# One written order for the first four chunks of a chunked recurrence followed by a two-matrix layer

## The chip, the cores and the metric

The kernel runs on one core of a Trainium2 chip. A time is device microseconds (us) for one execution of the whole program; smaller is better. TensorE is written PE in the profile, VectorE DVE, ScalarE ACT, GpSimd POOL and SyncE SP. PE's weight loads have their own row, PEld. SP computes nothing here: it issues DMAs, one after another, in the order of its instruction list.

## The reference

Two stages follow each other. The first is a recurrence over 768 tokens, with a 40 by 40 state for each of 4 batches and 8 heads:

```python
for t in range(S):
    y[:, :, t] = np.einsum('bhd,bhde->bhe', rt, state)
    Sa = np.einsum('bhde,bhe->bhd', state, at)
    state_decay = state * wt[:, :, None, :] - np.einsum('bhd,bhe->bhde', Sa, bt)
    state = state_decay + np.einsum('bhd,bhe->bhde', vt, kt)
```

Its output, turned to 3072 tokens by 320 channels, goes through a layer of two matrices with a SiLU between:

```python
h = x @ w_in                            # 320 x 2048
g = h * (1.0 / (1.0 + np.exp(-h)))
return (g @ w_out).astype(np.float32)   # 2048 x 320
```

The recurrence's inputs are float32. The two matrices arrive as float64, which the kernel has to turn into float32 itself.

## The kernel before, in words

**Chunks.** The 768 tokens are cut into twelve chunks of 64. A chunk has two units `m`, each with two of the four batches. Within a chunk the recurrence becomes matrix products around the inverse of a triangular 64 by 64 matrix for each head and batch; from chunk to chunk only the state `GV` is carried.

**What a chunk needs.** `prepare` scales it (two scans and a reciprocal on DVE for each unit, L335 and L336; key products on POOL) and forms the `scores` (PE products `pm`, evicted by DVE into `sb`, L286). The scores go through DRAM (`md`) into a layout with one matrix per partition (`mi`). `inverse` then solves row by row on DVE: a product `tmp` (L419) and a sum into `XI` (L426) for every row. The result returns through DRAM (`xd`) into `XT`. `merge` turns it (L463) and completes the inverse of size 64 from blocks with PE products (`corners`, `complete`, `first`, `second`). Chunks 0 and 1 are inverted one by one on 64 partitions, the later ones in pairs on 128 partitions; for chunks 0 to 3 the row solve goes to blocks of 16, later to blocks of 32.

**The chain of a chunk** has six steps for each unit: `keys` (products `pt`), `right` (`pr`), `solve` (`pu`, `pw`), `read` (`pl`, masked by DVE into `vl`, L722), `write` (`pgy`, then DVE's update of `GV`, L761 and L765, and `yx`, L770) and `turn` (`GT`). `keyed` makes a further masked product for the chunk (L308). The outputs of two chunks go to DRAM as `xs`.

**The layer.** For two chunks, 512 tokens, `moe` gives a queue of steps: `first` (products `ph` with `w_in`, L813 and L818, SiLU on ACT at L820) and `second` (products `po` with `w_out`, L825). For the first pair `first` is cut in two halves of 256 tokens, so that chunk 0's tokens can go ahead of chunk 1's. Such steps fill PE between the dependent products of a chain.

**The weights.** 40 pieces (`pieces`), each a float64 block of 128 partitions by 256 numbers. `load_weights` brings piece n into a free room; `weights(n)` does two bit operations of piece n on DVE (L178, L179), gives three conversions to ACT (L180 to L182), and finishes piece n - 1 with three DVE operations (L187, L189, L190). The first 20 pieces use five rooms inside parts of the weight tensors that are not written yet and the tile `room`; pieces 20 to 29 have three rooms, and the last ten the tiles `mi`, `tmp` and `room`. The tile tag `room` also holds `stage`, the keys of every odd chunk from 5 on (`staged`, `load`); `stack` copies them to where `keyed` wants them.

**Order.** Without further word the order within each engine is chosen when the program is built, from the order in which the steps are written and the buffers' lifetimes. `in_order` adds a dependency that costs nothing on the chip but fixes an instruction behind the last one given the same name: `"moe"` for PE, `"vector"` for DVE, `"sync"` for SP. Before, DVE's line is written for chunks 0 and 1's scaling, masks, inversions and pieces 0 to 3; SP's line is written at the very start, dropped (`del issued["sync"]`) and taken up again ahead of chunk 4. PE's line is kept for the layer's products, and from chunk 4 on (`mark["pair"]`, read by `product`) for all products. Chunks 0 to 3 are spread by `weave`, which mixes lists of steps evenly: the chain, the layer's steps, and the conversions. From chunk 4 a loop over pairs of chunks (L1025) states every step's place; `take(n)` runs the next n steps of the layer's queue.

Of the kernel before, what the change touches and what calls it, by code (L numbers as in the profile page):

```python
# [41 lines left out]
def kernel(  # L42
# [97 lines left out]
    def load_weights(done):  # L140

        while len(rooms) < NW:
            n = len(rooms)

            if n < NW // 2:
                place = ("wi0", "wi1", "wo0", "wo1", "room")[n % 5]
            elif n < NW * 3 // 4:
                place = ("wo0", "wo1", "room")[(n - NW // 2) % 3]
            else:
                place = ("mi", "tmp", "room")[(n - NW // 2) % 3]  # L150
            if taken.get(place, -1) > done:
                return
            taken[place] = n
            at = int(place[-1]) if place[0] == "w" else None
            if place[:2] == "wi":
                rooms[n] = wi_s[:, at, DF // 2 : DF // 2 + 4 * WS].bitcast(I32)
            elif place[:2] == "wo":
                at = NF * DM // 2 + 4 * WS * at
                rooms[n] = wo_f[:, at : at + 4 * WS].bitcast(I32)
            else:  # L160
                rooms[n] = sb.tile([128, 4 * WS], I32, name="room", tag=place)
            for lo, hi, src in pieces[n][1]:
                raw = rooms[n][lo:hi, 0 : 2 * WS]
                send(nc.sync, raw.rearrange("p (i x) -> p i x", x=256) if len(src.shape) == 3 else raw, src)
            if n < 3:
                return
# [6 lines left out]

    def weights(n, pin=lambda x: x, more=True):

        if n < NW:
            lo, hi, e, f = parts(n)
# [23 lines left out]
    def in_order(x, line="moe"):  # L201

        if line in issued:
            behind(x, issued[line])
        issued[line] = x.ins

    class Unit:
# [61 lines left out]
    def between(u, s):  # L269
# [15 lines left out]
        for j in range(2):  # L285
# [5 lines left out]
            )  # L291
            if u.n < 2:
                in_order(x, "vector")

    def keyed(u):
# [10 lines left out]
        for j in range(2):  # L306
# [6 lines left out]
            )  # L313
            if u.n == 0:
                in_order(x, "vector")

# [8 lines left out]
    def pre(u, md):  # L325
        def scale():
            u.W = sb.tile([128, Q, C + 1], F32, name="W", bufs=6)
            R = u.w[:, :, 1 : C + 1]
            pin = partial(in_order, line="vector") if u.n < 2 else lambda x: x
            if "pair" in mark and u.n % 2 == 0:  # L330

                pin = lambda x: behind(x, mark["row" if u.m == 0 else "across"])
# [61 lines left out]
    def inverse(md, N, queue, lo=0, hi=128):  # L394
# [18 lines left out]

        pin = partial(in_order, line="vector") if hi - lo == 64 else lambda x: x

# [26 lines left out]
    def merge(n, xd, queue):  # L442
# [14 lines left out]

        pin = partial(in_order, line="vector") if n < 2 else lambda x: x

# [138 lines left out]
    def chain(u, xs):  # L598
# [109 lines left out]
        def read():  # L708
# [12 lines left out]
            for j in range(2):  # L721
                nc.vector.tensor_tensor(  # L722
                    out=u.vl[:, :, j, D:],
                    in0=pl[j].rearrange("p (q t) -> p q t", q=Q),
                    in1=ml.unsqueeze(1).to_broadcast([128, Q, C]),
                    op=ALU.mult,
                )

        def write():
# [27 lines left out]
            for be in range(0 if last else 2):  # L757
                for j in range(2):
                    J = slice(DP * j, DP * j + DP)
                    g = gv[J, j, P * be : P * be + P]  # L760
                    nc.vector.tensor_tensor(out=g, in0=gy[be][J, :, 0:D], in1=g, op=ALU.add)  # L761
            for j in range(0 if last else 2):
                J = slice(DP * j, DP * j + DP)
                g = gv[J, j]
                nc.vector.tensor_tensor(  # L765
                    out=g, in0=g, in1=u.W[J, :, C : C + 1].to_broadcast([DP, Q, D]), op=ALU.mult
                )
            yx = sb.tile([128, P, 2, C], F32, name="yx")
            for be in range(2):
                nc.vector.tensor_tensor(  # L770
                    out=yx[:, :, be], in0=gy[be][:, :, D:], in1=u.W[:, P * be : P * be + P, 0:C], op=ALU.mult
                )
            at = 2 * C * (NM * (u.n % 2) + u.m)
# [10 lines left out]
    def moe(n0, xs, apart=False):  # L784
# [63 lines left out]
        for half in range(2):  # L848
            for c in range(2 if apart else 1):
                T = slice(W * c, W * c + W) if apart else slice(0, 2 * W)  # L850
                steps += [partial(first, T, NF // 4 * half + i) for i in range(NF // 4)]
                steps += [partial(second, half, b) for b in range(T.start // 128, T.stop // 128)]
        return fetch, steps
# [42 lines left out]
    for t in GVf + GT + XT + [x[DP * j + 32 : DP * j + DP, :, 1] for x in VUT for j in range(2)]:  # L896
        nc.gpsimd.memset(t, 0.0)
    def pinned(n, more=True):
        weights(n, partial(in_order, line="vector"), more)

# [10 lines left out]
    load_weights(-1)  # L911
    convert = [partial(weights, n) for n in range(NW + 1)]
    xs = dr.tile([DM, 4 * NM * C], F32, name="xs", bufs=2)
    steps = prepare(0)
    run([steps[i] for i in (0, 1, 4, 5)])
    pinned(0, False)
    pinned(1, False)
    run([steps[i] for i in (2, 6, 3, 7)])
# [13 lines left out]
    for u in units[0]:  # L932
        load_r(u)
    chains = {0: [chain(u, xs) for u in units[0]]}
    run(rows[1:18])
    for u in units[0]:
        keyed(u)
    run([x[i] for i in range(2) for x in chains[0]])
    run([next_steps[i] for i in (1, 2, 5, 6, 3, 7)])
    pinned(2)  # L940
    pinned(3)
    for u in units[1]:
        load_v(u)
    merge0 = late.pop(0)
    run(merge0[0:1])
    rows = invert(1, 1)
    run(rows[0:5] + merge0[1:2] + rows[5:9] + merge0[2:3] + rows[9:18] + merge0[3:])
    del issued["sync"]
    steps = [x for pair in zip(*[x[2:] for x in chains[0]]) for x in pair]
    steps[6:6] = late.pop(1)  # L950
    steps[2:2] = [partial(keyed, u) for u in units[1]]
    weave(steps, convert[4:12])
    for u in units[1]:
        load_r(u)
    for u in units[2] + units[3]:
        load(u)
    fetch, queue = moe(0, xs, True)
    fetch(0)
    steps = [x for pair in zip(*[chain(u, xs) for u in units[1]]) for x in pair]
    weave(steps[0:4], convert[12:14])  # L960
    issued["moe"] = mark["right"].ins
    weave(steps[4:], queue[0:4], convert[14:21])
    del queue[0:4]
    fetch(1)
    ahead = [prepare(n) for n in (2, 3)]
    weave(
        queue[0:8],
        [x[i] for x in ahead for i in (0, 5, 1, 6, 2, 7, 4, 9, 3, 8)] + [partial(keyed, u) for u in units[2]] + invert(3),
        convert[21:31],
    )  # L970
    del queue[0:8]
    for n in range(2, 4):
        for u in units[n]:
            load_v(u)
            load_r(u)
        for u in units[n + 2]:
            load(u)
        if n % 2 == 0:
            xs = dr.tile([DM, 4 * NM * C], F32, name="xs", bufs=2)
        steps = [x for pair in zip(*[chain(u, xs) for u in units[n]]) for x in pair]  # L980

        now = {2: 4, 3: 5}[n]
        x = prepare(n + 2)
        if n == 2:
            weave(steps[0:4], queue[0:1], [x[i] for i in (0, 5, 1, 6)], convert[31:34])
            scores = [x[i] for i in (2, 4, 7, 9, 3, 8)]
        else:
            weave(steps[0:4], queue[0:1], [x[i] for i in (0, 5, 2, 7, 1, 6, 4, 9, 3, 8)])
            scores = [partial(stack, u) for u in units[n + 2]]
        rows = invert(n + 2)  # L990
        merges = rows[35:]
        weave(
            steps[4:6] + late.pop(n, []) + [partial(keyed, u) for u in units[n + 1]] + steps[6:],
            queue[1:now],
            scores + rows[0:36],
            convert[34:] if n == 2 else [],
        )
        del queue[0:now]
    for u in units[6]:
        load(u, "bk")  # L1000
    fetch, more = moe(2, xs)
    fetch(0)
    queue += more

    def each(what, n, *x):
        for u in units[n] if n < NN else []:
            what(u, *x)

    def take(n):
        x = queue[0:n]  # L1010
        del queue[0:n]
        run(x)

    def start(n):

        x = [chain(u, xs) for u in units[n]]
        return [[y[i] for y in x] for i in range(len(x[0]))]


    mark["pair"] = True  # L1020
    issued["sync"] = mark["mi"]
    each(load_v, 4)
    each(load_r, 4)
    take(8)
    for n in range(4, NN, 2):  # L1025
        xs = dr.tile([DM, 4 * NM * C], F32, name="xs", bufs=2)
        keys, right, solve, read, write, turn = start(n)
        x = prepare(n + 2)
        later = late.pop(n)
        run(merges[1:2] + keys + merges[2:3] + right)  # L1030
        each(load_v, n + 1)
        each(load, n + 2, "a")
        each(load, n + 3)
        take(1)
        run(solve[0:1] + later[0:2] + [x[i] for i in (0, 5, 1, 6) if x])
        take(1)
        run(solve[1:2] + later[2:3] + [x[i] for i in (2, 7, 3, 8) if x] + read)
        each(load_vut, n + 1)
        take(1)
        run([x[i] for i in (4, 9) if x] + write)  # L1040
        each(load_vl, n + 1)
        each(keyed, n + 1)
        take(1)
        x = prepare(n + 3)
# [10 lines left out]
        rows = invert(n + 3)  # L1055
        merges = rows[35:]
        run(rows[0:1] + [x[i] for i in (3, 8) if x])
# [170 lines left out]
```

## Time and profile before

| | |
|---|---|
| Median of 3 runs | 901.02 us (898.65 to 906.04) |
| The profiled execution | 901.06 us, its span 899.2 us |
| PE busy / PEld busy | 778.9 (87%) / 552.9 (61%) us |
| DVE busy | 557.9 (62%) us |
| ACT / POOL busy | 297.4 (33%) / 151.4 (17%) us |
| Granted PE clock, mean | 0.946 of full speed |
| A reciprocal L336 / a row product of size 31 by 31, L419 | 3347 / 1160 ns |
| One `po` product L825 / one `ph` product L813, mean | 448 / 549 ns |

The span is the time from the first to the last instruction; some 1.9 us lie around it. A line of the timeline gives start, duration, engine, source line, operation, output and inputs, and in brackets how long the engine had been idle and what ended that. A line of the waits gives engine and product, what it waited for, and the total, the number of times and the longest in us. Most PE products of the chains carry L264, the line of the helper `product`; the tile's name tells them apart.

### The profile page before, as it was taken

To read this page: it belongs to the slowest core of one execution; us is meant where nothing else is said; L and a number is where in the kernel's file an instruction comes from. 1 tells how busy PE (TensorE), PEld (TensorE's weight loads), DVE (VectorE), ACT (ScalarE), POOL (GpSimd) and SP (SyncE) were. 2 spreads that over 40 slices of the span, in tenths; PEclk is the share of its full clock that TensorE was granted. 3 is DMA by queue.
4 is the path that set the end of the run, shared out by engine and by line. 5 is a ranking of instruction groups with operands and counts; after the bars stand their busy time and mean duration, and the time that the engine had idled before them with its cause. 6 is when DMAs were issued, how large, how long until landed. Compare 5 with 4: busy or idle time off the path is not lost.

```text
span 899.2 us, 25358 instructions
## 1 busy us (share of the span) xinstructions
PE 778.9 (87%) x10914; PEld 552.9 (61%) x10914; DVE 557.9 (62%) x1084; ACT 297.4 (33%) x689; POOL 151.4 (17%) x156
## 2 busy tenths in 40 slices
PE   2145689896898997999998999999999989999995
PEld 2135677674786853875746857648757468574643
DVE  9979889885439598176896295982768912510000
ACT  2234358532622322514025342226140243311120
POOL 7312024200202201303102240113031000000001
PEclk9999869996759998999999999999999999999998
DMA  7875646744325542444613627325424021102001
GB/s 154 167 147 142 150 130 150 166 106 107 90 59 128 105 110 47 115 108 87 145 34 62 157 64 158 93 48 117 96 56 122 16 61 40 42 23 57 1 1 33
DMA packets 240151, 82.99 MB, mean 92 GB/s; under 512 B 207136, under 2 KB 231968, under 8 KB 240032
## 3 DMA queue, kind: packets, MB, share of 16 engines
q1 hardware_dynamic: 219488, 69.96, 34.8%
q10 hardware_dynamic: 20544, 11.34, 4.7%
q8 instruction: 87, 1.43, 0.7%
q14 instruction: 32, 0.26, 0.1%
HBM read 67.11 MB, written 14.16 MB: 90 GB/s over the span
## 4 chain that ended last, share of the span: by engine, by line
PE 45%; DVE 19%; DMA 3%; SPq 2%; issue 1%; ACT 1%; POOL 0%; POOLq 0%; ACTq 0%; DVEq 0%
PE po L825 14%; PE ph L813 9%; DVE tmp L419 7%; DVE XI L426 7%; PE pgy L264 4%; PE pl L264 3%; PE ph L818 3%; PE pm L264 2%; SPq L217 2%; PE pt L264 2%; PE pr L264 2%; PE po L264 2%; PE pq L264 2%; PE pu L264 2%; DVE GV L761 1%
## 5 line engine op out<-in xcount | busy, mean ns | idle before, releaser
L825 PE MATMUL po<-wo_s,gts 128*128 128x320 f32 x768 | 224.8, 448 | 17.1 <-ACT gts L820 10.8
L825 PEld LDWEIGHTS po<-wo_s,gts 128*128 128x128 f32 x768 | 145.2, 194 | 82.7 <-ACT gts L820 14.7
L813 PE MATMUL ph<-xt,wi_s 128*128 128x512 f32 (+1 forms) x448 | 182.2, 549 | 2.2 <-ACT ot L834 1.4
L813 PEld LDWEIGHTS ph<-xt,wi_s 128*128 128x128 f32 x448 | 82.1, 192 | 82.3 <-issue 67.9
L820 ACT ACTIVATE gts<-ph 128x512 f32<-128x512 f32 (+1 forms) x112 | 54.6, 531 | 161.1 <-PE ph L818 160.4
L722 DVE TENSOR_TENSOR vl<-pl,ml 128x512 f32<-128x512 f32 x48 | 30.9, 685 | 113.0 <-PE pl L264 77.6
L419 DVE TENSOR_TENSOR tmp<-XI,mi 64x2 f32<-64x2 f32 (+40 forms) x169 | 85.5, 506 | 8.8 <-DMA mi<-md 3.9
L841 POOL TENSOR_TENSOR ot<-gts,ot 128x320 f32<-128x320 f32 x24 | 21.8, 907 | 358.1 <-ACT gts L839 352.9
L336 DVE RECIPROCAL w<-W 128x512 f32<-128x512 f32 x24 | 80.3, 3347 | 1.3
L426 DVE TENSOR_REDUCE XI<-tmp 64x2 f32<-64x2 f32 (+40 forms) x169 | 77.0, 455 | 5.2
L264 PE MATMUL pq<-XT,sb 32*32 32x32 f32 (+1 forms) x1280 | 34.9, 207 | 32.6 <-DVE XT L463 21.1
L818 PE MATMUL ph<-xt,wl_s 64*128 64x512 f32 (+1 forms) x224 | 56.9, 585 | 0.0
L264 PE MATMUL pm<-a,kb 64*64 64x64 f32 x1280 | 41.5, 244 | 16.9 <-POOL kb L366 15.5
L264 PEld LDWEIGHTS pq<-XT,sb 32*32 32x32 f32 (+1 forms) x1280 | 31.6, 131 | 38.7 <-issue 16.0
L363 POOL TENSOR_TENSOR a<-a,W 64x512 f32<-64x512 f32 x32 | 39.5, 1236 | 75.4 <-DMA a<-in_aT 52.2
L1084 DVE TENSOR_SCALAR bad<-pb 1x1 int32<-1x1 f32 x1 | 0.1, 147 | 83.4 <-PE pb L1083 83.4
L264 PEld LDWEIGHTS pm<-a,kb 64*64 64x64 f32 x1280 | 38.1, 156 | 21.2 <-POOL kb L366 15.7
L839 ACT COPY gts<-po 128x320 f32<-128x320 f32 x24 | 10.2, 425 | 121.8 <-PE po L825 98.0
L264 PEld LDWEIGHTS pl<-r,vut 64*128 64x128 f32 x768 | 45.4, 189 | 4.7 <-ACT vl L650 2.1
L264 PE MATMUL pl<-r,vut 64*128 64x64 f32 x768 | 46.5, 274 | 2.0 <-ACT vl L650 2.0
L264 PE MATMUL pt<-ident,kb 128*128 128x128 f32 x192 | 29.1, 313 | 21.2 <-DVE a L308 21.2
L348 POOL TENSOR_TENSOR kb<-kb,w 128x512 f32<-128x512 f32 x20 | 24.8, 1238 | 131.9 <-DVE w L336 118.6
(108 smaller groups left out, 1060.7 us busy)
## 6 DMA issues: line engine op xcount, KB each, us to landing
kb<-in_bT SPq DMA_DIRECT2D x48, 128.0 KB
vut<-in_vT SPq DMA_DIRECT2D x48, 128.0 KB
r<-in_rT SPq DMA_DIRECT2D x24, 256.0 KB
w<-in_wT SPq DMA_DIRECT2D x45, 128.0 KB
kb<-in_kT SPq DMA_DIRECT2D x44, 128.0 KB
a<-in_aT SPq DMA_DIRECT2D x32, 128.0 KB
vl<-in_v SPq DMA_DIRECT2D x48, 80.0 KB
xs<-yx ACTq DMA_DIRECT2D x48, 80.0 KB
```

The lines of the kernel that those rows point to most:

```text
L264: x = what(*x, **y)
L336: pin(nc.vector.reciprocal(R, u.W[:, :, 1 : C + 1]))
L348: nc.gpsimd.tensor_tensor(out=u.kb[:, :, 1], in0=u.kb[:, :, 1], in1=R, op=ALU.mult)
L363: nc.gpsimd.tensor_tensor(out=u.a[J, j], in0=u.a[J, j], in1=u.W[J, :, 0:C], op=ALU.mult)
L419: x = nc.vector.tensor_tensor(out=part, in0=X[L, :, t + 1 : N, t + 1 : N], in1=M[L, :, t, t + 1 : N].unsqueeze(2).to_broadcast([hi - lo, I ...
L426: x = nc.vector.tensor_reduce(out=X[L, :, t + 1 : N, t], in_=part, axis=AX.X, op=ALU.add)
L722: nc.vector.tensor_tensor(out=u.vl[:, :, j, D:], in0=pl[j].rearrange("p (q t) -> p q t", q=Q), in1=ml.unsqueeze(1).to_broadcast([128, Q, C ...
L813: in_order(nc.tensor.matmul(ph[n], lhsT=wi_s[:, k, at : at + 128], rhs=xt[:, k, :], start=k == 0, stop=False))
L818: in_order(nc.tensor.matmul(ph[n], lhsT=wl_s[R, i, :], rhs=xt[R, 2, :], start=False, stop=True))
L820: nc.scalar.activation(out=place(2 * i + n)[:, T], in_=ph[n], func=AF.Silu)
L825: in_order(nc.tensor.matmul(po[:, 0:DM], lhsT=place(f)[:, b * 128 : b * 128 + 128], rhs=wo_s[:, NF // 2 * half + f, :], start=f == 0, stop ...
L841: nc.gpsimd.tensor_tensor(out=ot4, in0=rest, in1=ot4, op=ALU.add)
```

## The change

Line numbers in the diff are those of the file before and after.

1. The order of PE, DVE and SP is written out from chunk 0. `mark["pair"]` is set before chunk 0's chain, so all products follow the written line of PE. A new `mark["front"]` holds until chunk 2's chain begins; while it does, `vec` puts each of DVE's steps, conversions too, into the line `"vector"`. SP's line is no longer dropped.
2. The weaves of chunks 0 to 3 are gone. Chunks 0 and 1 have a written list; chunks 2 and 3 run through the loop over pairs, which now starts at 2. `cv(n)` calls `weights(n)` at stated places.
3. `second` of the first pair comes after both halves of `first`.
4. The last ten pieces use two rooms, `mi` and `room`, and none is loaded into them until the row steps of chunks 2 and 3 have been written (`mark["rows"]`).
5. In the loop's first turn the loads of chunk 5 (`each(load, n + 3)`), `stage` among them, come after the last conversion.

```diff
@@ load_weights
-                place = ("mi", "tmp", "room")[(n - NW // 2) % 3]
+                place = ("mi", "room")[n % 2]
+                if "rows" not in mark:
+                    return
@@ new
+    def vec(x):
+        if "pair" not in mark or "front" in mark:
+            in_order(x, "vector")
+        return x
@@ moe: second behind both halves of first
-                steps += [partial(second, half, b) for b in range(T.start // 128, T.stop // 128)]
+            steps += [partial(second, half, b) for b in range(4)]
@@ the front, from chunk 0's chain to chunk 1's inversion
+    mark["pair"] = mark["front"] = True
+    keys, right, solve, read, write, turn = start(0)
+    run(rows[1:18])
+    each(keyed, 0)
+    run(keys + right)
+    cv(2)
...
+    first, rows = late.pop(0), invert(1, 1)
+    run(first[0:1] + rows[0:1])
+    cv(4)
+    run(first[1:2] + rows[1:6] + first[2:3] + rows[6:12] + first[3:5] + rows[12:17])
+    cv(5)
+    each(load, 3, "bk")
+    run(rows[17:18])
+    x = prepare(2)
+    run(solve + x[0:1])
+    cv(6)
+    then = late.pop(1)
+    run(then[0:2] + read)
...
+    run(keys + right)
+    each(load_v, 2)
+    each(load, 3, "a")
+    each(load, 4, "bk")
...
+    take(1)
+    run([y[4], y[9]] + turn)
+    rows = invert(3)
+    run(rows[0:1])
+    each(keyed, 2)
+    cv(14, 15, 16)
+    take(1)
+    cv(17)
+    weave(rows[1:17], [partial(take, 1)] * 3)
+    mark["rows"] = True
+    run(rows[17:19])
+    cv(18, 19, 20)
+    take(2)
+    cv(21, 22)
+    run(rows[19:20])
+    take(1)
+    merges = rows[20:]
+    del mark["front"]
@@ the loop over pairs
-    for n in range(4, NN, 2):
+    for n in range(2, NN, 2):
...
-        each(load, n + 3)
+        if n > 2:
+            each(load, n + 3)
         take(1)
+        if n == 2:
+            cv(*range(23, 30))
...
+        if n == 2:
+            cv(*range(30, 36))
...
         each(keyed, n + 1)
+        if n == 2:
+            cv(*range(36, NW + 1))
+            each(load, n + 3)
         take(1)
```

## The prediction

> **What bounds the kernel now.** I read the slices of the page first, then busy time by stage, then waits, then the timeline around the inversions.
>
> The slices, 22.5 us each; rows TensorE, VectorE and TensorE's granted clock:
>
> ```profile
> PE   2145689896898997999998999999999989999995
> DVE  9979889885439598176896295982768912510000
> PEclk9999869996759998999999999999999999999998
> ```
>
> VectorE is full over the first nine slices, TensorE from about the fifteenth on. The end of the program is TensorE alone. So the span is TensorE's work plus its holes, and the holes lie early. By stage (span, then busy us of TensorE, its weight loads, VectorE, ScalarE, GpSimd; clock, DMA):
>
> ```profile
> 0.00:125.00 125.00, 53.92 (x1480) 50.34 (x1481) 112.34 (x230) 43.99 (x104) 39.44 (x48) 0.92 0.69 157
> 125.00:205.00 80.00, 74.94 (x933) 57.58 (x929) 70.85 (x156) 48.19 (x123) 15.51 (x13) 0.95 0.52 124
> 205.00:265.00 60.00, 46.62 (x1262) 38.76 (x1260) 22.80 (x53) 24.25 (x58) 7.18 (x8) 0.63 0.36 90
> 265.00:350.00 85.00, 79.67 (x943) 55.76 (x942) 71.92 (x143) 21.28 (x51) 13.34 (x14) 0.98 0.41 94
> 357.00:804.00 447.00, 437.25 (x6032) 302.55 (x6033) 273.80 (x500) 143.14 (x319) 67.61 (x65) 0.98 0.37 83
> 804.00:889.00 85.00, 84.89 (x274) 47.04 (x272) 0.83 (x3) 13.12 (x27) 5.16 (x6) 1.00 0.09 23
> ```
>
> Chunks 0 and 1 (0 to 125) cost 71 us of TensorE's idling, 205 to 265 another 13 and a clock of 0.63: there chunks 2 and 3 are merged, VectorE is busy only 23 of 60 us, and both wait for weights:
>
> ```profile
> PE po L825 <- DVE wo_s L190: 6.3, 2, 3.7
> DVE room L178 <- DMA room<-in_w_out: 12.4, 6, 3.3
> ```
>
> From 357 TensorE misses 10 us in 447. So only what is done before chunk 4's inverse arrives can change the time much. Its path:
>
> ```profile
> 205.58 0.39 SPq L217 DMA_DIRECT2D room<-in_w_out  x1
> ...
> 208.60 0.29 DVE L178 TENSOR_SCALAR room<-room 128x256 int32<-128x256 int32 x1 [2.41 <-DMA room<-in_w_out]
> ...
> 286.15 1.49 POOL L359 TENSOR_TENSOR stage<-stage,W 128x512 f32<-128x512 f32 x1 [2.18 <-DVE W L335]
> 295.58 0.91 PE L264 MATMUL pm<-stage,kb 64*64 64x64 f32 x32
> 296.56 0.76 DVE L286 TENSOR_TENSOR sb<-pm,ms 128x256 f32<-128x256 f32 x2 [2.04 <-PE pm L264]
> 310.00 0.14 DVE L419 TENSOR_TENSOR tmp<-XI,mi 128x1 f32<-128x1 f32 x1
> 355.98 0.31 PE L264 MATMUL pq<-XT,sb 32*32 32x32 f32 x2 [3.68 <-DVE XT L463]
> ```
>
> A weight piece takes 3.0 us from issue to first use. Chunk 5's keys (`stage`) were loaded long before; its scores end at 297.3, the row steps begin at 310.0, and their result is used at 356.5 (the middle of its two first uses, 355.98 and 357.02).
>
> **What the Trainium skill says.** "Perfetto Trace Analysis", Tensor Engine Instruction: ACT, DVE and GpSimd are strict FIFO. So a conversion that waits for its load holds all VectorE work written behind it; the 2.41 us above agrees. "DMA: Bandwidth & Descriptors", Anatomy of one DMA: any semaphore wait happens on the issuing sequencer before dispatch. So a load that waits for its room holds every later load of SyncE; the 18.08 us that three `room` issues took from 215.88 agree. "TensorE: Matmul & The Clock Gate", Why this matters for your kernels: gaps above some 3 us put the array back to half clock; slices of 0.50 follow such gaps here (215 to 235, 245 to 265).
>
> **Part by part.**
>
> *Pinned row steps of chunk 1.* Before, they ran from 63.4 to 92.2, mixed with conversions and a reciprocal of 3.35. Alone they take what chunk 0's took, 30.8 to 43.8: 13 us; with `qq` (0.5) and the addition (0.9) they end near 76, 16 us sooner. SyncE in its written order has piece 9's load (free only after conversion 5, near 79) and eight `kb` loads at 0.65 ahead of chunk 1's fetch: issued 86 to 87.5, transposes end near 91 instead of 110.4. Price: chunk 0's `vl` and `GV` are now queued behind these transposes and end near 112 instead of 106.7. Chunk 1's `pr` comes near 125 instead of 131.
>
> *Fewer conversions ahead of the inversion of chunks 2 and 3.* From 112 VectorE has three scale steps (4.65 each: 14.0), ten conversions (two at 0.28, three at 0.42, 1.8: 18.0), two scores (2.8), `vl` (2.6), `GV` and `yx` (6.2), `keyed` (2.8): 46.4, and some 8 of waiting for chunk 2's scores, which TensorE now runs behind chunk 1's second solve. Rows begin near 167 and end near 181 instead of 205.6. **Lead: 24 us.**
>
> *What eats the lead.* In the built order VectorE has, between rows and chunk 2's transposes, conversions of pieces 20 to 23, whose loads are issued after the fetches of `XT`, pieces 22 and 23 only when 19 and 20 are done. Copy to first use was 10 us before (205.6 to 215.7), so chunk 3's transposes are near 191, and three more piece times (3.0 of load, and conversion) put chunk 2's near 201 to 204. Then 9 us of conversions and a scale step stand ahead of chunk 2's `qq` (213), and `qq` of chunk 3, behind chunk 2's solve in TensorE's written order, stops VectorE from 217 to about 230. Pieces 25 and up are queued on SyncE behind eight `GV` and four `a` loads that wait for chunk 2's `pr`. From 30 on there are two rooms, not three: load 3.0, conversion 1.8 and ScalarE's 1.4 make some 6.5 per pair. `vl` of chunk 2 stands behind piece 33. I put the end of chunk 2's `GV` at 265.5, against 277.2: lead **11.7**.
>
> *The added wait that decides.* `stage` of chunk 5 has the same memory as `room`, and is now loaded after piece 39. VectorE's list from chunk 2's `GV` to piece 39: two scale steps with reciprocals 9.5, sixteen `GT` transposes at 0.43 6.9, `keyed` and `yx` 3.6, four conversions 7.2, some 1 of waiting: 28, to 293.5. Load 3.1; GpSimd's product, two copies and key product 1.3, 1.2, 1.24: 300.4 for the first unit; with the first unit's other product the second follows 5.0 later, 305.4; scores and eviction 1.8: **307.2 against 297.3**. TensorE's order has chunk 3's read and write and four `ph` steps behind these scores; it stands from about 282 (`keyed` of chunk 3 near 270, then its `pr`, two `ph` steps and the two solves, some 12). Then four matmul steps of 2.6, 3.8, 2.6, 5.5 and VectorE's `GV`, `keyed`: 20.5, rows from 327.7; undisturbed they take 39 less 5.7 of `GV` work that was mixed in: 33.3, to 361; and 7.2 as before (349.3 to 356.5): **368.2 against 356.5, +11.7**.
>
> *MoE work put off.* Counted in the trace up to 357: `po` x144 of 16 a step and `ph` of 24 steps, thus 29 steps of the queue taken. The new order has taken 11 before its loop and 16 in the first turn: 27. Two are late, one `ph` of 512 columns (3.63+1.06) and one `po` (4.50): **9.2**. They fall into the tail, which has no hole to hide them.
>
> *Nothing charged:* the hint-only dependencies of the written order; they cost no instruction. Removing `tmp` as a room is in the 6.5 per pair. If that cover is wrong it shows as piece time.
>
> Sum: profiled execution 901.06 (span 899.2, 1.9 around it; the median of the three runs is 901.02) +11.7+9.2 = **922**.
>
> Unknown costs: the lead at chunk 2's write, from 0 (11.7 later than reckoned: 934) to the full 24 (12.3 earlier: 910); piece time in two rooms, from the 3.0 seen to the 5.1 between 208.60 and 213.73: ten pieces, up to +17. A gain is not excluded, as below.
>
> **Rivals.**
> - *No change.* `stage` comes in time: if pieces keep near VectorE's own 1.8, the room chain gives back some 12, and with half the lead kept chunk 4's inverse is 8 early: 901-8+9.2 = 902. For: VectorE was idle 37 of the 60 us up to 265, so there is space. Against: the idle time there is made of waits that remain.
> - *Faster*, the other side: the lead of 24 made by the pinned rows reaches chunk 4's inverse whole, since TensorE always has a MoE step to run between products: 901-24+9.2 = 886. It decides from a lead of 18.2 at that inverse. For: 90 us of TensorE's idling up to 265 (71+5+13). Against: the conversions, 36 for pieces 20 to 39, must then fit beside 31 us of rows.
> - *Worse*: strict orders stop each other in turns (SyncE for a room, VectorE for that load, TensorE for VectorE): the piece time of 5.1 holds, +17: 939.
>
> **How the numbers follow.** Forecast 0.52, around 911 to 932; no change 0.20; faster 0.13; worse 0.15. Two measurements of this kernel can tell about 1% apart, 892 to 910. So faster 0.13, same 0.20, slower 0.67. Range: leaving out the faster case and the far end of the worse one, 897 to 938.
>
> **What would show it.** Right: chunk 1's transposes near 91; rows of chunks 2 and 3 ended near 181; TensorE idle before `pm` from `stage` for 20 us or more; GpSimd's first wait for `stage` ended by its DMA; chunk 4's first use of `XT` near 368; two more MoE steps in the tail. Wrong: no hole before the scores of chunk 5, or that first use before 350.

## The result: 940.0 us, and the profile after

The changed kernel takes 940.04 us (median of 4 runs, 937.63 to 942.83), the kernel before 900.54 in the same comparison: a ratio of 1.0429, 95% interval 1.0374 to 1.0484. The forecast was 922, with a range to 938: the direction is right, the size is not, and the measured time lies 2 us above the range. The profiled execution took 937.63 us, its span is 935.8, against 899.2 before: 36.6 us more.

The slices of the page after, TensorE, VectorE and TensorE's clock, are now 23.4 us each:

```profile
PE   3063887847686399599997999989999999999996
DVE  9967588784479279619598176894487922410000
PEclk9975679867798599799999999999999999999998
```

By stage (span, then busy us of TensorE, its weight loads, VectorE, ScalarE, GpSimd; clock, DMA):

```profile
0.00:125.00 125.00, 59.18 (x1557) 54.44 (x1558) 96.13 (x183) 37.74 (x88) 37.41 (x46) 0.77 0.63 137
125.00:205.00 80.00, 53.36 (x765) 41.49 (x764) 67.10 (x146) 37.79 (x95) 14.85 (x12) 0.84 0.51 125
205.00:265.00 60.00, 44.58 (x1201) 36.43 (x1200) 28.48 (x70) 30.65 (x75) 9.24 (x10) 0.76 0.25 70
265.00:350.00 85.00, 59.38 (x986) 48.59 (x983) 57.52 (x141) 26.18 (x69) 10.23 (x11) 0.84 0.52 119
804.00:889.00 85.00, 85.00 (x557) 50.28 (x554) 7.49 (x16) 17.04 (x37) 3.45 (x4) 1.00 0.09 22
889.00:935.80 46.80, 38.78 (x124) 20.76 (x123) 0.15 (x1) 6.47 (x13) 3.45 (x4) 0.95 0.08 16
```

TensorE works 21.6 us less than before from 125 to 205 (74.94 to 53.36) and 20.3 less from 265 to 350 (79.67 to 59.38). That work comes back at the end: 38.8 us of it lie behind 889, where the kernel before has none. No stage from 0 to 350 has TensorE busier by more than 5.3.

The lines that answer to the path of chunk 4's inverse, from the timeline after:

```profile
191.76 0.58 DVE L443 COPY mi<-XI 128x512 f32<-128x512 f32 x1
...
205.41 3.72 SPq L226 DMA_DIRECT2D wo_s<-in_w_in  x2
...
220.45 0.39 DVE L491 TENSOR_SCALAR qq<-pq,lower 128x256 f32<-128x256 f32 x1
...
233.50 5.44 SPq L226 DMA_DIRECT2D GV<-in_v  x8
238.99 2.58 SPq L226 DMA_DIRECT2D a<-in_aT  x4
241.68 0.53 SPq L226 DMA_DIRECT2D room<-in_w_in  x1
...
242.25 0.48 DVE L491 TENSOR_SCALAR qq<-pq,lower 128x256 f32<-128x256 f32 x1 [16.12 <-ACT vut L678]
...
267.99 0.69 DVE L729 TENSOR_TENSOR vl<-pl,ml 128x512 f32<-128x512 f32 x1
...
279.06 1.34 DVE L768 TENSOR_TENSOR GV<-pgy,GV 64x160 f32<-64x160 f32 x4
...
308.66 0.38 SPq L226 DMA_DIRECT2D stage<-in_aT  x1
315.44 1.13 PE L273 MATMUL pm<-stage,kb 64*64 64x64 f32 x32 [17.90 <-POOL kb L355]
343.65 0.14 DVE L426 TENSOR_TENSOR tmp<-XI,mi 128x1 f32<-128x1 f32 x1
384.58 0.31 PE L273 MATMUL pq<-XT,sb 32*32 32x32 f32 x2 [8.70 <-DVE XT L470]
```

and three lines of the timeline before that they are set against:

```profile
220.61 0.48 DVE L484 TENSOR_SCALAR qq<-pq,lower 128x256 f32<-128x256 f32 x1 [1.24 <-PE pq L264]
...
264.93 3.99 PE L264 MATMUL pl<-r,vut 64*128 64x64 f32 x64
...
276.17 1.01 DVE L765 TENSOR_TENSOR GV<-GV,W 64x320 f32<-64x320 f32 x2
```

The inverse of chunks 2 and 3 is copied 13.8 us sooner than before (191.76 against 205.58): the front does give a lead. At chunk 2's `qq` hardly any of it is left (220.45 against 220.61): seven pieces and two scale steps on VectorE come between the two, and on TensorE most of three `po` steps, which wait for the pieces. Then SyncE issues no weight piece between 209.1 and 241.7: its next issues are chunk 3's `GV` rows and chunk 4's `a`, which wait for chunk 2's `pr`, and the pieces are behind them. VectorE stands for 16.1 us, to 242.25. Chunk 2's `pl` still begins 1.9 us sooner than before (263.0 against 264.9), but `vl`, which reads it, comes on VectorE behind piece 33, and chunk 2's update of `GV` ends 4.2 later than before (281.4 against 277.2). Chunk 5's `stage` is loaded at 308.7, behind the last piece; TensorE stands for 17.9 us before the scores. The two first uses of chunk 4's `XT` are at 384.6 and 385.9, the middle 385.3, against 356.5. What follows takes 550.5 us (935.8 - 385.3) against 542.7 (899.2 - 356.5). So +28.8 lies before that use and +7.8 behind it.

### The profile page after: what moved, and what is told of

Read it like the earlier page. It is cut to its first block, busy times and chain, and to the rows that moved or that the text cites. A ratio compares the mean times of both kernels' runs of the same rounds, so it can differ in the third digit from the quotient of the medians.

```text
span 935.8 us, 25352 instructions
## 1 busy us (share of the span) xinstructions
PE 770.8 (82%) x10914; PEld 547.2 (58%) x10914; DVE 557.0 (60%) x1084; ACT 298.3 (32%) x689; POOL 150.9 (16%) x156
## 4 chain that ended last, share of the span: by engine, by line
PE 43%; DVE 22%; DMA 4%; SPq 2%; ACT 2%; issue 1%; POOL 1%; POOLq 0%; DVEq 0%; ACTq 0%
PE po L832 14%; PE ph L820 10%; DVE tmp L426 7%; DVE XI L433 6%; PE pgy L273 4%; PE ph L825 3%; PE pl L273 3%; PE pt L273 2%; SPq L226 2%; PE pr L273 2%; PE pq L273 2%; PE pu L273 1%; DVE w L343 1%; PE pm L273 1%; DVE a L316 1%
## 5 line engine op out<-in xcount | busy, mean ns | idle before, releaser
L832 PE MATMUL po<-wo_s,gts 128*128 128x320 f32 x768 | 218.1, 441 | 13.7 <-DVE wo_s L193 13.7
L820 PE MATMUL ph<-xt,wi_s 128*128 128x512 f32 (+1 forms) x448 | 184.5, 555 | 14.0 <-ACT gts L827 11.5
L832 PEld LDWEIGHTS po<-wo_s,gts 128*128 128x128 f32 x768 | 144.8, 192 | 78.7 <-DVE wo_s L193 16.1
L273 PE MATMUL pq<-XT,sb 32*32 32x32 f32 (+1 forms) x1280 | 27.7, 202 | 34.6 <-DVE XT L470 28.6
L273 PEld LDWEIGHTS pl<-r,vut 64*128 64x128 f32 x768 | 47.8, 201 | 2.5 <-issue 1.9
L273 PEld LDWEIGHTS pq<-XT,sb 32*32 32x32 f32 (+1 forms) x1280 | 24.4, 124 | 41.6 <-issue 21.2
L273 PE MATMUL pl<-r,vut 64*128 64x64 f32 x768 | 48.4, 285 | 0.1
L841 ACT COPY ot<-po 128x320 f32<-128x320 f32 x24 | 10.1, 423 | 109.8 <-PE po L832 84.5
```

The lines of the kernel that those rows point to most:

```text
L273: x = what(*x, **y)
L820: in_order(nc.tensor.matmul(ph[n], lhsT=wi_s[:, k, at : at + 128], rhs=xt[:, k, :], start=k == 0, stop=False))
L832: in_order(nc.tensor.matmul(po[:, 0:DM], lhsT=place(f)[:, b * 128 : b * 128 + 128], rhs=wo_s[:, NF // 2 * half + f, :], start=f == 0, stop ...
```

## The experiments

The kernel before was run along with every group: medians 901.4 to 902.5. Where a time is set against the changed kernel, that is 940.0; the kernel before had 900.5 beside it, so such a difference is uncertain by 1 to 2 us on top of the runs' scatter. All kernels compute the whole of the reference.

**Early keys.** Chunk 5's `stage` in the memory of `tmp`, loaded before the last conversions:

```diff
-mark["stage"] = sb.tile([128, NM, Q, C], F32, name="stage", tag="room")
+mark["stage"] = sb.tile([128, NM, Q, C], F32, name="stage", tag="tmp" if u.n == 5 else "room")
             cv(*range(30, 36))
+            each(load, n + 3)
...
             cv(*range(36, NW + 1))
-            each(load, n + 3)
```

(and `stack` of chunk 5 ahead of its inversion, so that `tmp` is free for it)

> The changed kernel with chunk 5's keys (`stage`) in the memory of `tmp`, which lies idle between the two inversions, loaded ahead of the last conversions; nothing is left out. Theory that the wait for `room` decides: scores of chunk 5 come as soon as GpSimd's products allow, near 303 instead of 322.3, TensorE's hole of 17.9 us ahead of them goes, and the program takes 18 to 20 us less, near 921. Rival, that the lost lead at chunk 2's write is what counts and the wait only falls into the same hole: VectorE's scale steps and conversions end at 297 to 308 anyhow, under 6 us are gained, 935 or more.

Measured 937.1 (ratio to the kernel before 1.0408, 1.0365 to 1.0451): 2.9 less, hardly to be told from the changed kernel. One half of the theory came true and the other did not. The scores came 12.5 us sooner (evicted at 309.8 against 322.3) and TensorE's idle time ahead of them went. But:

```profile
314.96 5.80 SPq L226 DMA_DIRECT2D GV<-in_v  x8
...
326.71 2.95 SPq L226 DMA_DIRECT2D md<-sb  x4
329.77 0.49 SPq L226 DMA_DIRECT2D mi<-md  x1
...
338.61 0.16 DVE L426 TENSOR_TENSOR tmp<-XI,mi 128x1 f32<-128x1 f32 x1 [10.82 <-DMA mi<-md]
...
380.23 0.31 PE L273 MATMUL pq<-XT,sb 32*32 32x32 f32 x2 [21.20 <-DVE XT L470]
```

In SyncE's written order the way of the scores to DRAM stands behind the last pieces, chunk 4's `GV` rows and chunk 6's `kb`. The row steps waited 10.8 us for it and began only 5.0 sooner, and TensorE now stands for 21.2 us ahead of the first use of `XT` (8.7 in the changed kernel). One wait had hidden the next. Chunk 2's `GV` also ended 5.5 later here, at 286.9; its `pl` products took 7.09 us at a clock of 0.50, where the changed kernel has 3.79 at 1.00.

**Scores first.** The early keys, and SyncE's issues of chunk 5's scores ahead of chunk 4's `GV` and chunk 6's `kb`:

```diff
-        each(load_v, n + 2)
-        each(load, n + 4, "bk")
+        if n > 2:
+            each(load_v, n + 2)
+            each(load, n + 4, "bk")
...
-        run(rows[0:1] + [x[i] for i in (3, 8) if x])
+        run(rows[0:1])
+        if n == 2:
+            each(load_v, n + 2)
+            each(load, n + 4, "bk")
+        run([x[i] for i in (3, 8) if x])
```

> The kernel with chunk 5's keys loaded early, and in addition SyncE's issues of chunk 5's scores (`md`, `mi`) ahead of chunk 4's `GV` rows and chunk 6's `kb`; nothing is left out. With the early keys alone the scores were evicted at 309.8, but `md` was issued at 326.7 behind eight `GV` and eight `kb` issues, and the row steps waited 10.8 us for `mi`. Theory that the wait for `room` had only been followed by SyncE's order: `md` goes at about 315, the row steps begin near 323 instead of 338.6, chunk 4's first use of `XT` near 366, and the program takes 12 to 16 us less than with the early keys alone, 921 to 925. Rival, that VectorE's `GV` and `keyed` work of chunk 3 (to 327.8) or the room of the last pieces holds the rows anyhow: they begin at 330 or later, 930 or more.

Measured 922.4 (1.0219, 1.0168 to 1.0271), 17.6 less than the changed kernel. `md` goes at 312.5, the row steps begin at 325.8, the first use of `XT` is at 367.7. The memory of `room` together with SyncE's order behind it is 17.6 of the 39 us.

**Two more steps of the layer** ahead of chunk 5's scores:

```diff
-        run(solve[1:2] + [x[i] for i in (4, 9) if x])
+        run(solve[1:2])
+        take(2 if n == 2 else 0)
+        run([x[i] for i in (4, 9) if x])
```

> The changed kernel with two more steps of the layer taken ahead of the scores of chunk 5, where TensorE stands for 17.9 us. Theory that the two steps put off are paid in full in the tail: the hole shrinks to about 12, the tail loses one `ph` step and one `po` step or two `po` steps, 8 to 9 us less, near 931.5. Rival, that the hole's end moves with what fills it, or that the steps are missed in the hole of 8.7 us ahead of chunk 4's `pq` instead: under 3 us gained, 937 or more.

Measured 932.6 (1.0331, 1.0283 to 1.0380), 7.4 less. In the timeline of this kernel the hole ahead of the scores is smaller, as expected, and so is the one ahead of `XT`:

```profile
320.11 1.13 PE L273 MATMUL pm<-stage,kb 64*64 64x64 f32 x32 [10.26 <-POOL kb L355]
...
391.19 0.31 PE L273 MATMUL pq<-XT,sb 32*32 32x32 f32 x2 [3.59 <-DVE XT L470]
```

The rival was right in part: the end of the hole moved too, by 4.7 us, and the first use of `XT` came 6.6 later. What follows that use became 10.9 shorter, which is more.

**Pieces first.** Chunk 3's `GV` and chunk 4's `a` behind pieces 25 to 31 on SyncE:

```diff
-        each(load_v, n + 1)
-        each(load, n + 2, "a")
         if n > 2:
+            each(load_v, n + 1)
+            each(load, n + 2, "a")
             each(load, n + 3)
         take(1)
         if n == 2:
             cv(*range(23, 30))
+            each(load_v, n + 1)
+            each(load, n + 2, "a")
```

> The changed kernel with chunk 3's `GV` rows and chunk 4's `a` issued behind pieces 25 to 31 on SyncE instead of ahead of them; nothing is left out. Theory that the lead of the front was lost because no piece was fetched from 209 to 241.7, while SyncE stood for chunk 2's `pr`, and VectorE stood with it for 16 us: pieces 25 to 29 are converted before 242, `GV` of chunk 2 ends at 270 to 274 instead of 281.4, the last piece at 298, the scores of chunk 5 near 312, and the program takes 8 to 11 us less, 929 to 932. Rival, that VectorE stands for chunk 3's `qq` all the same and the pieces wait behind it, or that the late `a` holds chunk 4's scores: within 3 us of 940.

Measured 930.1 (1.0294, 1.0248 to 1.0339), 9.9 less. The time is as the theory had it, the way isn't: `GV` of chunk 2 ends at 281.1, hardly sooner than 281.4, and the gain is in the pieces, and with them in chunk 5's keys (loaded at 302.1 instead of 308.7) and scores (evicted at 315.7 instead of 322.3).

**Three rooms** for the last ten pieces (`place = ("mi", "tmp", "room")[(n - NW // 2) % 3]`):

> The changed kernel with three rooms for the last ten pieces (`mi`, `tmp`, `room`) as before, still not filled until the row steps of chunks 2 and 3 are written. Theory that the two rooms cost 6.5 us for a pair of pieces: the ten pieces end some 5 to 8 us sooner than 308.6, chunk 5's keys come so much sooner, 932 to 935. Rival, that VectorE's other work between the pieces sets their pace: under 2 us, 938 to 941.

Measured 942.2 (1.0436, 1.0389 to 1.0483): no gain. The scores were evicted at 322.8. The time is nearer to the rival's, but the run does not settle what paces the last pieces, because the built order of VectorE became another: pieces 25 to 30 stand ahead of chunk 3's `qq`, which came at 260.3 instead of 242.2, and chunk 2's `GV` ended at 293.4, 12.0 later. In spite of that chunk 5's keys were loaded 7.1 sooner, at 301.6, as the theory had it. The scores did not follow, since VectorE had its last conversions and `GT` transposes ahead of them; six steps of these conversions took 0.82 to 1.40 us, others some 0.42. They ran while GpSimd worked on the keys; whether that slowed them was not tested.

**VectorE free in the front** (`vec` does nothing once `mark["pair"]` is set):

> The changed kernel without VectorE's written order in the front; TensorE's and SyncE's stay. Theory that the pinned row steps of chunk 1 bring the gain that the change has: chunk 1's rows end near 85 to 92 instead of 75.8, the rows of chunks 2 and 3 some 10 us later than 180.4, the program 5 to 10 us slower, 945 to 950. Rival, that VectorE's written order costs more than it brings, since what it holds back lets TensorE stand: 930 or less.

Measured 943.6 (1.0442, 1.0385 to 1.0499): not to be told from the changed kernel. Yet the front changed much. The timeline of this kernel:

```profile
93.77 0.60 DVE L443 COPY mi<-XI 64x512 f32<-64x512 f32 x1
...
205.81 0.60 DVE L443 COPY mi<-XI 128x512 f32<-128x512 f32 x1
...
246.73 0.48 DVE L491 TENSOR_SCALAR qq<-pq,lower 128x256 f32<-128x256 f32 x1 [5.82 <-PE pq L273]
...
284.39 1.34 DVE L768 TENSOR_TENSOR GV<-pgy,GV 64x160 f32<-64x160 f32 x4
```

Chunk 1's inverse is copied 18.6 us later than with the written order (75.2), that of chunks 2 and 3 14.0 later; at chunk 3's `qq` 4.5 are left of it, at chunk 2's `GV` 5.3, in the time 3.6, which the intervals do not tell from nothing. In this run a lead of the front is worth about a quarter of itself.

**Extra products in TensorE's hole** from 78.3 to 90.4, written behind chunk 0's solve (`warm(42)`: products of `ident` with `one` into an unused bank):

> The changed kernel with 42 extra products into an unused bank, written between chunk 0's solve and chunk 1's merge, where TensorE stood idle for 12.1 us (77.9 to 90.4); they add work that nothing reads. Theory that the idle stretch of TensorE, made by the pinned row steps, halved its clock and so lost part of the lead: the `pl` products of chunk 0 take 3.8 us instead of 7.1, `pm` 2.0 instead of 3.6, `pgy` 2.8 instead of 4.1; chunk 0's `GV` ends some 5 us sooner than 117.8, the rows of chunks 2 and 3 start near 175 instead of 180.4, and the program takes some 4 to 6 us less, 934 to 936. Rival, that later waits for weights swallow it: rows start earlier, the total stays at 940.

Measured 946.8 (1.0505, 1.0468 to 1.0543), 6.7 more than the changed kernel, though the two intervals just overlap and the profiled execution took 939.8. The size of the edit was wrong: a float32 product leaves two records in the trace (84 for these 42), so that the duration of one record was taken for that of a product; the 42 took 19.4 us, not ten, and chunk 1's `qq` came 4 us later. They did keep the clock, 0.92 from 90 to 112 where the changed kernel has 0.51: the `pl` products behind them took 3.79 us instead of 7.09, and chunk 0's `GV` ended at nearly the same time in spite of the delay (118.4 against 117.8). That the idle stretch cost clock is shown; what it is worth at the end is not.

**Chunk 2's transposes first**, ahead of pieces 20 to 22 and of three `po` steps:

```diff
     run(rows[17:19])
-    cv(18, 19, 20)
+    cv(18, 19)
+    run(rows[19:22])
+    cv(20)
     take(2)
     cv(21, 22)
-    run(rows[19:20])
     take(1)
-    merges = rows[20:]
+    merges = rows[22:]
```

> The changed kernel with chunk 2's transposes, its `qq` and the addition that follows ahead of pieces 20 to 22 on VectorE and ahead of the layer's three `po` steps on TensorE; nothing is left out. Theory that the written order itself spends the lead here: the inverse is copied at 192.3, but chunk 2's transposes end at 212.1 behind four pieces and its `qq` comes at 220.5; with the edit the transposes end near 203, `qq` comes near 205, SyncE's stand for chunk 2's `pr` ends some 12 us sooner than 233.5, and the program takes 8 to 14 us less, 926 to 932. Rival, that the pieces set the pace and the time comes back as VectorE's wait for chunk 3's `qq`: 936 or more.

Measured 940.9 (1.0445, 1.0400 to 1.0490): nothing. `qq` came at 207.6 instead of 220.5, SyncE's stand ended at 231.7 instead of 233.5, because TensorE's order now has the three `po` steps (24 products, 15.9 us) between chunk 2's `qq` and its `pr`.

Of chunk 2's late write two accounts were left: SyncE's stand, or TensorE's order, in which chunk 3's merge stands between the two solves of chunk 2 and its read. Two runs were to take them away one at a time.

**SyncE's stand taken away**: GpSimd issues chunk 3's `GV` rows and chunk 4's `a`:

```diff
-        each(load_v, n + 1)
-        each(load, n + 2, "a")
+        each(load_v, n + 1, nc.gpsimd if n == 2 else nc.sync)
+        each(load, n + 2, "a", nc.gpsimd if n == 2 else nc.sync)
```

> The changed kernel with chunk 3's `GV` rows and chunk 4's `a` issued by GpSimd, so that SyncE does not stand for chunk 2's `pr`; nothing is left out. Theory that SyncE's stand (no piece issued from 209 to 241.7) is what sets the end of chunk 2's write and of the pieces: pieces 25 to 31 are issued from about 212 on, VectorE does not stand 16 us for chunk 3's `qq`, chunk 4's scores are not later than 273, and the program takes 9 to 13 us less, 927 to 931. Rival, that TensorE's order sets it: `GV` of chunk 2 ends at 280 as before, only the last pieces come sooner, 934 or more.

Measured 930.4 (1.0302, 1.0267 to 1.0336), 9.7 less. The timeline of this kernel:

```profile
226.77 0.33 SPq L226 DMA_DIRECT2D wo_s<-in_w_in  x1
227.16 34.50 SPq L226 DMA_DIRECT2D room<-in_w_out  x7
...
244.74 0.48 DVE L491 TENSOR_SCALAR qq<-pq,lower 128x256 f32<-128x256 f32 x1
...
275.57 1.30 DVE L768 TENSOR_TENSOR GV<-pgy,GV 64x160 f32<-64x160 f32 x4
...
301.43 0.38 SPq L226 DMA_DIRECT2D stage<-in_aT  x1
```

VectorE no longer stands before chunk 3's `qq`, though that comes no sooner; it converts pieces in that time. `GV` of chunk 2 ends at 277.9, 3.5 sooner, and chunk 5's keys are loaded 7.2 sooner. The time is the theory's, the way only in part: chunk 2's `pl` begins at 262.0, 1.0 sooner than in the changed kernel, so up to there the stand does not set chunk 2's chain. As with pieces first, the gain comes by the last pieces and the keys.

**Chunk 3's merge later**, behind chunk 2's read (for n == 2 the steps of `later` move behind `read`):

> The changed kernel with chunk 3's merge behind chunk 2's read in the written orders, instead of between the two units' solves; nothing is left out. Theory that TensorE's order sets chunk 2's write: VectorE's 16 us of waiting for chunk 3's `qq` go, `pl` comes near 246 instead of 263 and chunk 2's `GV` near 262, 16 sooner, and the program takes 8 to 14 us less, 926 to 932. Rival, that chunk 3 then comes as much later as chunk 2 comes sooner, and the pieces, which wait for SyncE, set the rest: within 4 us of 940.

Measured 937.0 (1.0380, 1.0337 to 1.0424), 3.0 less: the rival's range. VectorE then stood 20.2 us for piece 25, whose load was still behind SyncE's stand, in place of the 16.1 for `qq`:

```profile
246.47 0.67 DVE L181 TENSOR_SCALAR room<-room 128x256 int32<-128x256 int32 x1 [20.18 <-DMA room<-in_w_in]
```

Chunk 2's `pl` began at 245.4, as the theory had it. But the merge, now behind the read, still stands ahead of the write in TensorE's order, and `GV` ended at 287.2, 5.8 later. So this run does not clear TensorE's order, and both waits were not taken away together.

**All edits together** (scores first, pieces first, three rooms, two steps):

> The changed kernel with all of it together: chunk 5's keys early in `tmp`'s memory, its scores ahead of chunk 4's `GV` on SyncE, pieces 25 to 32 ahead of chunk 3's `GV` and chunk 4's `a`, three rooms for the last ten pieces, and two more steps of the layer ahead of chunk 5's scores. If each gain is on the chain and they add (3 measured for the early keys, 12 to 16 for SyncE's order, 8 to 11 for the pieces, 7.5 measured for the two steps), the program takes 905 to 912. Rival, that they share one limit (VectorE's 36 us of conversions beside 31 us of rows): 920 or more.

Measured 909.0 (1.0083, 1.0057 to 1.0109): within the first theory's 905 to 912.

**And chunk 2's transposes first in addition:**

> The kernel with all edits together (909.0 measured) and in addition chunk 2's transposes, `qq` and addition ahead of pieces 20 to 22 and of the three `po` steps. Theory that chunk 2's chain is what is late: `GV` of chunk 2 ends 8 or more earlier than 276.3, chunk 4's first use of `XT` comes at 355 to 358 instead of 366, and the program takes 897 to 902, as before the change or below it. Rival, that the last pieces, converted one by one in two or three rooms, set chunk 5's scores (298 to 301) and so the rest: 905 or more.

Measured 905.2 (1.0051, 1.0030 to 1.0071), still some 0.5% slower than before. `GV` of chunk 2 ends at 272.8, the first use of `XT` is at 361.2. Neither theory's numbers hold quite; the time is the rival's.

**The same with `GV` and `a` further ahead** (in the trace behind piece 27 instead of 32):

> The same kernel as the last, but with chunk 3's `GV` rows and chunk 4's `a` issued behind piece 28 and not behind piece 32 on SyncE. Theory that with chunk 2's chain early, the loads that wait for its `pr` stand little: within 2 us of the kernel before it in this list. Rival, that chunk 4's late `a` holds its scores and so the rows: 3 to 6 us faster than it.

Measured 916.8 (1.0172, 1.0129 to 1.0216): 11.7 slower than the one before it, outside both. Five pieces behind SyncE's stand are enough: VectorE waited 9.98 us for the first of them.

**The same with GpSimd's queue** in place of pieces first:

> The kernel with all edits and chunk 2's transposes first (905.2 measured), but with chunk 3's `GV` rows and chunk 4's `a` issued by GpSimd in place of being put behind the pieces on SyncE. Theory that the late `a` (240.8) then was the last wait left between 206 and 265: chunk 4's scores come some 5 us sooner, 898 to 902, at or below the kernel before. Rival, that the conversions of the pieces fill VectorE there whichever queue brings the loads: 904 to 907.

Measured 907.9 (1.0062, 1.0044 to 1.0081): not better than 905.2, and just above its rival's range. No kernel of this study is faster than the one before.

**The kernel before with pinned row steps alone:**

```diff
-    convert = [partial(weights, n) for n in range(NW + 1)]
+    convert = [partial(pinned, n) if n < 12 else partial(weights, n) for n in range(NW + 1)]
```

> The kernel before the change with one part of it alone: conversions 4 to 11 are pinned on VectorE behind chunk 1's row steps, which so run undisturbed. Theory that a lead from the front is spent where the pieces are converted: chunk 1's inverse ends near 77 instead of 92.2, chunk 1's transposes come some 10 us sooner than 107.5, and yet the program's time is within 4 us of 901. Rival, that such a lead reaches chunk 4: 887 to 893.

Measured 909.9 (1.0107, 1.0055 to 1.0159), slower, and its first step was missed: chunk 1's inverse is copied at 87.0, not 77, and its transposes begin at 111.2, later than the 106.7 of before; the inverse of chunks 2 and 3 is copied at 215.2 instead of 205.6. So it doesn't say what a lead is worth. That pieces held back early are missed later would fit it, but was not tested further.

The profiled executions put in one table. First use is the middle of the first two `pq` of chunk 4, the rest is the span less that:

| kernel | span | first use of `XT` | rest | layer steps taken by then |
|---|---|---|---|---|
| before | 899.2 | 356.5 | 542.7 | 29 |
| changed | 935.8 | 385.3 | 550.5 | 27 |
| early keys | 933.8 | 380.9 | 552.9 | 27 |
| scores first | 919.1 | 367.7 | 551.4 | 27 |
| SyncE's stand taken away | 929.4 | 378.4 | 551.0 | 27 |
| two steps | 931.5 | 391.9 | 539.6 | 29 |
| all and transposes first | 903.0 | 361.2 | 541.8 | 29 |

The first use and the rest make the span by definition. What the table shows is that the rest falls into two groups: 550.5 to 552.9 where 27 steps were taken, 539.6 to 542.7 where 29 were, thus some 8 to 13 us for two steps.

## Why the prediction was wrong, by its own steps

**Right: pinned row steps of chunk 1.** Inverse near 76, transposes to 91 were expected; they end at 75.8 and 92.4. The price was sized too low: chunk 0's `GV` ended at 117.8, not 112. TensorE stood for 12.1 us from 78.3, and its clock was 0.51 from 90 to 112 (before: 0.84); the `pl` products took 7.09 us at a clock of 0.50, where they take 3.79 at 1.00. The prediction cites the Trainium skill for this ("TensorE: Matmul & The Clock Gate", Why this matters for your kernels: a long gap between products puts the array back to half clock) and left it out of this sum. Of its two examples in the kernel before, the second, from 245 on, follows a gap of 2.58 us, not one above 3.

**A miss, though a later or earlier inverse changed little: fewer conversions.** Rows of chunks 2 and 3 from 167 to 181 were expected; they run from 180.4 to 191.8, a lead of 13.8 instead of 24. The late `GV` above may be some 6 of the 11 us missed. But with VectorE free the same copy came 14 us later for 3.6 us of time, and with chunk 2's `qq` 13 us sooner the time did not move: in these runs neither a shorter lead nor a longer one changed the result much.

**The step that failed: what eats the lead.** The prediction put the end of chunk 2's `GV` at 265.5, a lead of 11.7, and bounded it from below by a lead of nothing (934). Measured: 281.4, 4.2 later than before. This error of 15.9 is nearly all of the 17.1 at the first use of `XT` (385.3 against 368.2). The step reckoned a chain of fixed length, 84.5 us from the end of the inverse to `GV`, so that a lead at its start is kept less the additions. It measured 89.6, from an inverse that ended 10.8 later than put (191.8 against 181). In the sum, then, 11 of the 16 come in with the inverse and 5 with the stretch.

But the runs show that the stretch has no fixed length. With the copy 14.0 later, `GV` was 5.3 later; with chunk 2's `qq` 12.9 sooner, it was no sooner; with the transposes first added to all edits, `qq` came 16.0 sooner and `GV` 4.5. What stands there in place of the chain is work that the change took from the front and wrote behind it: in the kernel before VectorE had begun 34 of the 40 pieces by 211 and 38 by 242, after it 24 and 25. Part of it lies ahead of chunk 2's `qq`, where the lead ends; the rest is behind SyncE's stand, named by the prediction, in which for 32 us no piece is issued. Taking that stand away gave 3.5 us at `GV` and 9.7 in the time. How the remaining 12 at `GV` divide between TensorE's order and the pieces stays open: moving chunk 3's merge gave 3.0 in the time, no more than the measurement can tell, and left the merge ahead of the write.

**Right in size, incomplete in kind: the added wait.** From chunk 2's `GV` to the end of chunk 5's scores 41.7 us were expected and 40.9 measured; from there to the first use of `XT` 61.0 and 63.0; TensorE idle 20 or more, and 17.9 + 3.7. The wait is there. But it did not decide alone: with the keys early 2.9 us came back, with SyncE's order of `md` changed too 17.6. The forecast put the 20.5 us between scores and rows down to TensorE's products and VectorE's `GV` of chunk 3, and did not look at what SyncE has ahead of `md`; once the keys came early, it was that which held the rows.

**Right: MoE work put off.** 29 steps before (9 of `po` and 20 of `ph`; the prediction's 24 of `ph` is a miscount, its 29 is not), 27 after, 9.2 us into the tail expected; the rest grew by 7.8, and two steps taken earlier gave 7.4.

**The rival named worse** gave 939, and the time is 940; that is in part luck. It charged the whole +17 to the last ten pieces, at 5.1 us each with SyncE standing for a room. (From the 6.5 for a pair, ten pieces at 5.1 are 18.5 more, not 17.) Those ten did take 5.4 us each, from 254.4 to 308.6, with VectorE's other work between them, and SyncE did stand for a room, from 289.5 to 302.1. But the error was there before them, at chunk 2's `GV`, and from `GV` to the scores the forecast's 41.7 held; three rooms brought the keys sooner and no time. What it had right is that the written orders stop one another in turns: SyncE for TensorE, VectorE for SyncE's load.

**The other rivals.** The lead did not reach chunk 4 whole (886), and `stage` did not come in time (902).

The gains of scores first (17.6), of pieces first (9.9) and of the two steps (7.4) make 34.9. The kernel with all edits and transposes first is 34.9 below the changed one; that the two agree so well is chance, for without the transposes it is 31.0. What is left to the kernel before is 3.3 us between the medians.

## What to carry to other kernels

When loads, spills and prefetches share one issuing engine in a written order, look at each issue that waits for a late product and list what is queued behind it: that list can set when the next stage starts, as much as the chain of computing engines. An early result is worth only as much as the next wait lets through, so follow a lead to each point downstream (here copy 13.8, `qq` 0.2, `pl` 1.9, `GV` -4.2) before adding it to a sum. When a wait is taken away, read what became last in its place before judging that it did not matter: here two waits lay on one another, and removing one of them gave a sixth of what both gave.

## What was not expected of the hardware

Each float32 product is two records in the trace: 42 products of 128x128 with 128x260 are 84 records and took 19.36 us, 0.46 each; the layer's products of 128x256 are 8 records for 4 products in 1.99 us, 0.50 each. A count of float32 products read from a row has to be halved. GpSimd's issue of a DMA took as long as SyncE's: eight `GV` rows in 5.03 us against 5.44; the time for it was there, since GpSimd had been idle for 11.7 us before.
